# The scores' maximum taken from SBUF, and a pair of PSUM banks held as two tiles

## The chip, the core and the metric

The kernel runs on one core of one Trainium2 chip. The metric is the device time of one execution in microseconds (us); the time of a kernel is the median of its runs. Engine names are those of the profile: PE is the tensor engine's matmul, PEld its weight load, DVE the vector engine, ACT the scalar engine, POOL GpSimd, SP the engine that issues transfers. A PSUM bank holds 512 float32 values in each of 128 partitions, and the kernel uses all eight.

## The reference

Two attentions follow each other per batch and head, then an expert layer follows. All data are float32, with 8 batches, 8 heads, 576 rows, head dimension 64, and 32 packed rows (`p`).

```python
def sm_attn(qq, kk, vv):
    s = scale * np.matmul(qq, kk.transpose(0, 1, 3, 2))
    s = s - np.max(s, axis=-1, keepdims=True)
    a = np.exp(s)
    a = a / (np.sum(a, axis=-1, keepdims=True) + 1e-09)
    return np.matmul(a, vv)
p_packed = sm_attn(p, k, v)
out = sm_attn(q, p_packed, p_packed)
```

The result, as 4608 tokens of 512 values, goes through `h = x @ w_in` (512 by 2048), `g = h * clip(h + 3, 0, 6) / 6` and `g @ w_out` (2048 by 512).

## The kernel before

**The work.** The kernel never forms the attention output. For each batch it makes M, the product of the packed rows and `w_in` (`u_m`), and multiplies it with the second attention's weights (`first_product`, L929) to get h. The gate (`gate_into`, L940 on ACT and L941 on DVE) and the second product with `w_out` (`product`, L969) follow. Float32 operands are parted into a high and a low part in a reduced format (`split`, L946 on ACT and L947 mostly on POOL), and three products of the parts stand for one. From the second chunk of batch 1 on, the second products of most slices go by pairs (`moe_pairs`) with sums of weights that `combine` (L1071 to L1095) makes during batch 1.

**The attention of a batch**, for batches 1 to 7, is a chain of generators. `u_s1` makes the scores of p against k. It has two halves of 288 columns and two parities of heads (`x`), so a half fills a pair of banks, one bank for each parity, with eight products (L350, in `each_head`). For each bank ACT copies the 288 columns to the SBUF tile `e` (L385), and DVE takes their maximum into one column of `mx` (L387). After both halves DVE joins the two maxima and scales them (L391), ACT takes the exponential in place (L398), and DVE makes the reciprocal of the sum (L402, L404). `u_ets` turns e with PE transposes (L440, copies L444), `u_pvs` multiplies with v (L470, L474), `u_ppt` turns the packed rows, and `u_s2` makes the second scores and their softmax (L494 to L524). `u_m` makes a quarter of M in a pair of banks and parts it (`m_hi` L537 on ACT, `m_lo` L539 on DVE).

**The banks.** In the steady stage four banks are accumulators (`ps_o`), two are h (`ps_h`), and two are the attention's pair (`ps_a`). That pair comes from `att_pair`, which in the steady stage gives the two halves of one tile of two banks under one tag with one buffer; before it, `att_pair` gives two separate one-bank tiles of a pool with two buffers. Where the scores' two halves are made at once (batch 1), the second pair is a two-bank tile of `ps_h0` (`ps_w`), the tile that also takes the next first product of `first_moe` (L607). A tile's buffer is handed on when all readers of the tile are done, and the build adds the semaphores.

**The order of the work.** The first stage (batch 0 and batch 1's attention, until the pools change) has its order on all five engines written out in `PLAN`: each token advances one generator by one `yield`. `S` tokens advance `u_s1` of batch 1, which makes both halves at once. The second half's banks come first there. After it, `fill` advances the next batch's attention by `STAGES` beside the expert steps of the present one, and the build's planner orders the instructions on each engine by a model of their times. Only the groups of L350 and L470 have their order on PE fixed, and `behind_gates` keeps what a fill issues behind the product and gate of the step. A quarter of `w_in` is fetched again for each `u_m` from batch 2 on (`w_again`, issued on SP), and a fetch waits until the quarter before has been read.

Of the kernel before, what the change touches and what calls it, by code (L numbers as in the profile page):

```python
# [10 lines left out]
F32 = mybir.dt.float32  # L11
# [5 lines left out]
ALU = mybir.AluOpType  # L17
AX = mybir.AxisListType
# [59 lines left out]
def packed_attention_moe(  # L78
# [17 lines left out]
    nc = tc.nc  # L96
    B, H, S, D = q.shape
    NPK = p.shape[2]
    DM, DF = w_in.shape
    P = 128  # L100
# [10 lines left out]
    scale = 1.0 / float(D) ** 0.5  # L111
# [119 lines left out]
    def att_ps():  # L231
        return spare_ps(0) if steady else ps_a.tile([P, 512], F32, name="ps1", tag="att")

    def att_pair():

        if not steady:
            return [att_ps() for _ in range(2)]
        t = ps_a.tile([P, 2, 512], F32, name="ps2", tag="att")
        return [t[:, x] for x in range(2)]

    state, steady = {}, []

# [93 lines left out]
    def each_head(rows, *rounds):  # L336

        banks = [spare_pair() if i else att_pair() for i in range(len(rounds))]  # L340
        with tc.manual_schedule(engines={mybir.EngineType.PE}), tc.high_priority():
            for pair, cols in reversed(list(zip(banks, rounds))):
                for a in (range(NPAIR - 1, -1, -1) if steady else range(NPAIR)):
                    for x in (1, 0):
                        half = slice(64 * x, 64 * x + 64)
                        c = cols(a, half)
                        n = 1
                        for m in c.shape[1:]:
                            n *= m
                        nc.tensor.matmul(  # L350
                            pair[x][NPK * a:NPK * a + NPK, :n], rows[half, a], c, start=True, stop=True
                        )
        return banks

    def scores(lhs, rhs, *halves):
        def cols(hf):
            hs = slice(hf * HS, (hf + 1) * HS)
            return lambda a, half: rhs[a][half].rearrange("p t i -> p (t i)")[:, hs]

        return [[s[:, :HS] for s in pair] for pair in each_head(lhs, *(cols(hf) for hf in halves))]  # L360

    def both_halves(at_once, lhs, rhs):

        if at_once:
            done = scores(lhs, rhs, 0, 1)
            yield None
            yield from ((hf, done[hf]) for hf in ((0, 1) if steady else (1, 0)))
        else:
            for hf in range(2):
                done = scores(lhs, rhs, hf)  # L370
                yield None
                yield hf, done[0]

    def u_s1(b):
        kt = [state.pop(("k", b, a)) for a in range(NPAIR)]
        pt = state.pop(("p", b))
        e = [ap.tile([P, NST * P], F32, name="e", tag="e", bufs=4) for _ in range(2)]
        mx = [sm.tile([P, 2], F32, name="mx") for _ in range(2)]
        for part in both_halves(b == 1, pt, kt):
            if part is None:  # L380
                yield 1
                continue
            hf, banks = part
            for x, s in enumerate(banks):
                nc.scalar.copy(out=e[x][:, hf * HS:(hf + 1) * HS], in_=s)  # L385
                yield 1
                nc.vector.reduce_max(out=mx[x][:, hf:hf + 1], in_=s, axis=AX.X)  # L387
                yield None if x else 1
        for x in range(2):
            nb = sm.tile([P, 1], F32, name="nb")  # L390
            nc.vector.tensor_scalar(  # L391
                out=nb, in0=mx[x][:, 0:1], scalar1=mx[x][:, 1:2], scalar2=-scale, op0=ALU.max, op1=ALU.mult
            )
            yield 1
            den = sm.tile([P, 1], F32, name="den")
            rinv = sm.tile([P, 1], F32, name="rinv")
            state["e", b, x] = (e[x], rinv)
            nc.scalar.activation(  # L398
                out=e[x][:, :S], in_=e[x][:, :S], func=AF.Exp, bias=nb, scale=scale, accum_out=den
            )  # L400
            yield
            nc.vector.tensor_scalar_add(den, den, 1e-9)  # L402
            yield 1
            nc.vector.reciprocal(rinv, den)  # L404
            yield 1
# [25 lines left out]
    def u_ets(b):  # L431

        e = [state["e", b, x][0] for x in range(2)]
        nc.vector.tensor_copy(out=e[0][:, S:], in_=e[1][:, 4 * P:S])
        yield 1
        et = [ap.tile([P, NST * P], F32, name="et", tag="e", bufs=4) for _ in range(2)]
        pair = att_pair()
        for x in range(2):
            for c in range(4):
                nc.tensor.transpose(  # L440
                    out=pair[x][:, c * P:(c + 1) * P], in_=e[x][:, c * P:(c + 1) * P], identity=ident
                )
            yield 1
            nc.scalar.copy(out=et[x][:, :4 * P], in_=pair[x])  # L444
            yield
        ps = att_ps()
        nc.tensor.transpose(out=ps[:, :P], in_=e[0][:, 4 * P:], identity=ident)
        yield 1
        nc.vector.tensor_copy(out=et[0][:, 4 * P:], in_=ps[:, :P])
        state["et", b] = et  # L450
        yield

    def u_pvs(b):

        rinv = [state.pop(("e", b, x))[1] for x in range(2)]
        et = state.pop(("et", b))
        low = state.pop(("v", b))
        high = [state.pop(("v_high", b, i)) for i in range(2)]
        pair = att_pair()
        rest = et[0][:, 4 * P:]  # L460
        with tc.manual_schedule(engines={mybir.EngineType.PE}), tc.high_priority():
            for c in range(NST):
                for x in range(2):
                    for a in range(NPAIR):
                        cols = slice(NPK * a, NPK * a + NPK)
                        if c < 4:
                            l, r = et[x][:, c * P:(c + 1) * P][:, cols], high[a // 2][:, a % 2, c] if x else low[:, a, c]
                        else:
                            l, r = rest[64 * x:64 * x + REM, cols], low[64 * x:64 * x + REM, a, c]
                        nc.tensor.matmul(pair[x][cols, :D], l, r, start=(c == 0), stop=(c == NST - 1))  # L470
        yield
        pn = state["pn", b] = ap.tile([P, 2, D], F32, name="pn", tag="pn", bufs=1)
        for x in range(2):
            nc.vector.tensor_scalar_mul(pn[:, x], pair[x][:, :D], rinv[x])  # L474
            yield 1
# [103 lines left out]
    def attention(b):  # L579

        yield from coarse(u_s1(b))
        turn("q", b, 0)
        load("q", b, 2)
        yield
        turn("q", b, 1)
        load("q", b, 3)
        yield
        yield
        turn("q", b, 2)
        load_v_high(b, 0)  # L590
        yield
        turn("q", b, 3)
        load_v_high(b, 1)
        yield
        yield from coarse(u_ets(b))
        yield from coarse(u_pvs(b))
        yield
        yield from coarse(u_ppt(b))
# [712 lines left out]
    def next_attention(chains, b):  # L1311


        def once(part):
            part()
            yield

        chains["lp"] = once(lambda: load_p(b))
        chains["tp"] = once(lambda: transpose_p(b))
        for a in range(NPAIR):  # L1320
            for which in "kq":
                chains[f"l{which}{a}"] = once(lambda which=which, a=a: load(which, b, a))
                chains[f"t{which}{a}"] = once(lambda which=which, a=a: turn(which, b, a))
        chains["S"] = u_s1(b)
        chains["lv"] = once(lambda: load_v_low(b))
        for i in range(2):
            chains[f"lw{i}"] = once(lambda i=i: load_v_high(b, i))
        chains["E"] = u_ets(b)
        chains["V"] = u_pvs(b)
        chains["T"] = u_ppt(b)  # L1330
        chains["Z"] = u_s2(b)
        chains["M"] = u_m(b, 0)
# [17 lines left out]
    with tc.manual_schedule(engines=HAND):  # L1350
        for name in PLAN.split():
            if name == "upper":
                upper.close()
                ps_a = upper.enter_context(tc.tile_pool(name="ps_a0", bufs=2, space=bass.MemoryType.PSUM))
# [11 lines left out]
    ps_a = ctx.enter_context(tc.tile_pool(name="ps_a", bufs=1, space=bass.MemoryType.PSUM))  # L1366
# [103 lines left out]
```

## Time and profile before

| what | value |
|---|---|
| time, median of 3 runs | 710.08 us (709.35 to 710.96) |
| the profiled execution's own time | 711.58 us |
| its span, first to last instruction | 709.8 us |
| PE busy | 690.0 us, 97% |
| PEld busy | 593.8 us, 84% |
| DVE busy | 531.0 us, 75% |
| ACT busy | 429.3 us, 60% |
| POOL busy | 354.5 us, 50% |
| chain that ended last, by engine | PE 87%, DVE 6%, DMA 3%, ACT 2% |
| mean granted PE clock | 0.99 |

A row of the timeline has the start in us, the duration in us, engine, line, operation, the tile written and the tiles read, their shapes, and in brackets the engine's idle time before it and what ended it. A row of the waits has the waiting engine, tile and line, what it waited for, the total in us, how often, and the longest. A row on a line's instructions has the shortest, the median and the longest duration in ns and the first and last start. PE's matmuls overlap, so the start of the next tells more than the end of the last.

### The profile page before, as it was taken

Reading aid. Unit: us, or ns where it says so; the run is one execution under the profiler, and the core shown is the slowest. Engines: PE = TensorE matmul, PEld = TensorE weight load, DVE = VectorE, ACT = ScalarE, POOL = GpSimd, SP = SyncE. Lnnn points to the kernel's source line nnn. Section 1 sums busy time; section 2 is a strip of 40 time slices with the busy share of each in tenths; the row PEclk is TensorE's granted clock in tenths of the full one; section 3 lists DMA queues with packets and bytes.
Section 4 is the critical chain, followed back from the end, with each engine's and each line's share of the span. In section 5 each row is a group of like instructions: output and inputs, shape, how many; then the busy total and the mean of one; then the engine's idle time right before and its main releaser. Section 6 shows DMA issues by size and latency. Waiting matters only on the chain.

```text
span 709.8 us, 16077 instructions
## 1 busy us (share of the span) xinstructions
PE 690.0 (97%) x5906; PEld 593.8 (84%) x5906; DVE 531.0 (75%) x1169; ACT 429.3 (60%) x1013; POOL 354.5 (50%) x539
## 2 busy tenths in 40 slices
PE   6699999999998999999999999999999999999997
PEld 5487876888877988899798998889888998889997
DVE  3888788687899769885598867888488867975453
ACT  4798876556556656566466655657366664756453
POOL 1455642555453454475453544556354444547553
PEclk9699999999999999999999999999999999999999
DMA  9969952955328655464454647375543745331030
GB/s 264 341 152 275 215 150 110 266 149 121 109 105 210 165 141 210 116 168 89 118 206 128 160 104 233 120 157 130 127 165 119 166 123 179 119 135 46 31 104 30
DMA packets 199102, 107.48 MB, mean 151 GB/s; under 512 B 173424, under 2 KB 185200, under 8 KB 195440
## 3 DMA queue, kind: packets, MB, share of 16 engines
q1 hardware_dynamic: 198480, 106.26, 53.9%
q8 instruction: 46, 0.75, 0.5%
q14 instruction: 32, 0.26, 0.1%
q10 hardware_dynamic: 544, 0.20, 0.1%
HBM read 89.65 MB, written 16.78 MB: 150 GB/s over the span
## 4 chain that ended last, share of the span: by engine, by line
PE 87%; DVE 6%; DMA 3%; ACT 2%; issue 1%; SPq 0%; POOL 0%; DVEq 0%; ACTq 0%
PE acc L969 47%; PE ps_hh L929 23%; PE ps L350 6%; PE ps_h L607 4%; PE ps L969 2%; PE ps L470 1%; DMA w_again<-w_kept 1%; PE ps L440 1%; DMA room<-in_moe_w_in_dram 1%; DVE wt L1076 1%; PE ps_t L678 1%; DMA k_nat<-in_k_dram 1%; PE ps L273 1%; DVE t L941 1%; PE ps_w L720 1%
## 5 line engine op out<-in xcount | busy, mean ns | idle before, releaser
L929 PE MATMUL ps_hh<-a_hi,m_hi 128*128 128x320 f32 (+1 forms) x448 | 133.8, 299 | 1.7 <-PE acc L969 0.8
L929 PE MATMUL ps_hh<-a_lo,m_hi 128*128 128x320 f32 (+1 forms) x448 | 133.4, 298 | 0.0
L929 PE MATMUL ps_hh<-a_hi,m_lo 128*128 128x320 f32 (+1 forms) x448 | 132.9, 297 | 0.0
L941 DVE SCALAR_TENSOR_TENSOR t<-t,ps_hh 128x320 f32<-128x320 f32 (+1 forms) x148 | 66.1, 446 | 60.3 <-ACT t L940 59.6
L947 POOL TENSOR_TENSOR gf<-tb,gf 128x256 fp32r<-128x256 f32 x76 | 64.3, 847 | 84.3 <-ACT gf L946 48.9
L969 PE MATMUL acc<-wo_hi,g 128*128 128x512 f32 x288 | 103.3, 401 | 0.0
L940 ACT ACTIVATE t<-ps_hh,three 128x320 f32<-128x320 f32 (+1 forms) x148 | 73.8, 500 | 37.3 <-PE ps_hh L929 30.0
L929 PEld LDWEIGHTS ps_hh<-a_hi,m_hi 128*128 128x128 f32 x448 | 84.6, 189 | 8.3 <-issue 3.0
L929 PEld LDWEIGHTS ps_hh<-a_lo,m_hi 128*128 128x128 f32 x448 | 84.7, 189 | 6.6 <-issue 3.5
L929 PEld LDWEIGHTS ps_hh<-a_hi,m_lo 128*128 128x128 f32 x448 | 84.6, 189 | 2.9 <-issue 2.5
L947 POOL TENSOR_TENSOR g<-t,g 128x256 fp32r<-128x256 f32 x72 | 56.3, 783 | 45.4 <-ACT g L946 26.2
L969 PE MATMUL acc<-wt,ga 128*128 128x256 f32 x456 | 74.1, 284 | 0.3 <-ACT ga L946 0.3
L969 PE MATMUL acc<-wo_hi,ge 128*128 128x256 f32 x304 | 71.3, 285 | 0.0
L947 POOL TENSOR_TENSOR ga<-t,ga 128x256 fp32r<-128x256 f32 x76 | 62.4, 821 | 13.9 <-ACT ga L946 12.6
L969 PEld LDWEIGHTS acc<-wt,ga 128*128 128x128 f32 x456 | 63.0, 190 | 2.7 <-ACT ga L946 1.5
L969 PEld LDWEIGHTS acc<-wo_hi,g 128*128 128x128 f32 x288 | 52.8, 188 | 13.9 <-POOL g L947 4.2
L969 PEld LDWEIGHTS acc<-wo_hi,ge 128*128 128x128 f32 x304 | 53.0, 190 | 7.9 <-DVE t L941 2.5
L965 POOL COPY bnd<-t 128x64 f32<-128x64 f32 x76 | 23.0, 302 | 70.8 <-DVE t L941 65.8
L969 PE MATMUL acc<-wo_lo,g 128*128 128x512 f32 x144 | 56.9, 395 | 0.0
L555 DVE STREAM_TRANSPOSE tr<-nat 128x576 f32<-128x576 f32 x56 | 42.3, 763 | 14.3 <-DMA nat<-in_q_dram 10.8
L940 ACT ACTIVATE tb<-ps_hh,three 128x256 f32<-128x256 f32 (+1 forms) x76 | 37.9, 498 | 21.8 <-PE ps_hh L929 19.8
L947 POOL TENSOR_TENSOR edge<-bnd,edge 128x256 fp32r<-128x256 f32 (+1 forms) x50 | 32.7, 659 | 32.5 <-ACT edge L946 32.5
(222 smaller groups left out, 1837.6 us busy)
## 6 DMA issues: line engine op xcount, KB each, us to landing
w_again<-w_kept SPq DMA_DIRECT2D x24, 1024.0 KB, 4.9
wt<-t_kept SPq DMA_DIRECT2D x24, 768.0 KB, 5.6
out_dram<-osb SPq DMA_DIRECT2D x33, 256.0 KB, 2.4
nat<-in_k_dram SPq DMA_DIRECT2D x112, 72.0 KB, 3.0
nat<-in_q_dram SPq DMA_DIRECT2D x112, 72.0 KB, 2.7
raw_in<-in_moe_w_in_dram SPq DMA_DIRECT2D x10, 512.0 KB, 5.7
raw_out<-in_moe_w_out_dram SPq DMA_DIRECT2D x10, 512.0 KB, 4.9
w_kept<-w_in_sb SPq DMA_DIRECT2D x4, 1024.0 KB, 9.2
```

Of the source, the lines that this page charges most:

```text
L273: nc.tensor.matmul(banks[x][NPK * a:NPK * a + NPK, :n * P], state["pp"][half, NPAIR * x + a], cols[half, :, a], start=True, stop=True,)
L350: nc.tensor.matmul(pair[x][NPK * a:NPK * a + NPK, :n], rows[half, a], c, start=True, stop=True)
L440: nc.tensor.transpose(out=pair[x][:, c * P:(c + 1) * P], in_=e[x][:, c * P:(c + 1) * P], identity=ident)
L470: nc.tensor.matmul(pair[x][cols, :D], l, r, start=(c == 0), stop=(c == NST - 1))
L555: nc.vector.transpose(out=t, in_=state.pop(("nat", which, b, a)))
L607: nc.tensor.matmul(h[:, hf, :HS], mm[:, g, fs], aa[:, hf * HS:(hf + 1) * HS], start=(g == 0 and i == 0), stop=(g == NG - 1 and i == 2),)
L929: state["first"] = nc.tensor.matmul(h[:, :n], mm[:, g, fs], aa[:, t0:t0 + n], start=(g == 0 and i == 0), stop=(g == NG - 1 and i == 2),)
L940: state["relu"] = nc.scalar.activation(out=t[:, :n], in_=h, func=AF.Relu, bias=three)
L941: state["gate"] = nc.vector.scalar_tensor_tensor(out=t[:, :n], in0=t[:, :n], scalar=6.0, in1=h, op0=ALU.min, op1=ALU.mult)
L947: engine.tensor_sub(out=lo, in0=x, in1=hi.bitcast(F32))
L965: nc.gpsimd.tensor_copy(out=bnd[:, f, side * REM:side * REM + REM], in_=t[:, boff:boff + REM])
L969: nc.tensor.matmul(out, lhs[x], rhs[y], start=first and i == 0, stop=last and i == 2, skip_group_check=True)
```

## The change

Three things change.

- `att_pair` gives, in the steady stage, two tiles of one bank with a tag of their own each (`att0`, `att1`), instead of the two halves of one tile of two banks. Users of the pair are `each_head` (scores and M), `u_ets`, `u_pvs` and, in the last batch, `edge_step`.
- `u_s1` no longer reads the banks with DVE. The copies to `e` stay. Once the second half of a parity is copied, one maximum over all 576 columns is taken from `e`. The number of `yield`s is the same, so a token of `PLAN` that took a maximum of the first copied half now issues nothing.
- The scaling of the maximum reads one column and multiplies by a constant.

```diff
         if not steady:
             return [att_ps() for _ in range(2)]
-        t = ps_a.tile([P, 2, 512], F32, name="ps2", tag="att")
-        return [t[:, x] for x in range(2)]
+        return [ps_a.tile([P, 512], F32, name="ps2", tag=f"att{x}") for x in range(2)]
...
         mx = [sm.tile([P, 2], F32, name="mx") for _ in range(2)]
+        copied = 0
         for part in both_halves(b == 1, pt, kt):
             if part is None:
                 yield 1
                 continue
             hf, banks = part
+            copied += 1
             for x, s in enumerate(banks):
                 nc.scalar.copy(out=e[x][:, hf * HS:(hf + 1) * HS], in_=s)
                 yield 1
-                nc.vector.reduce_max(out=mx[x][:, hf:hf + 1], in_=s, axis=AX.X)
+                if copied == 2:
+                    nc.vector.reduce_max(out=mx[x][:, 0:1], in_=e[x][:, :S], axis=AX.X)
                 yield None if x else 1
         for x in range(2):
             nb = sm.tile([P, 1], F32, name="nb")
-            nc.vector.tensor_scalar(
-                out=nb, in0=mx[x][:, 0:1], scalar1=mx[x][:, 1:2], scalar2=-scale, op0=ALU.max, op1=ALU.mult
-            )
+            nc.vector.tensor_scalar(out=nb, in0=mx[x][:, 0:1], scalar1=-scale, scalar2=None, op0=ALU.mult)
```

## The prediction

> **What bounds the kernel now.** I read the page's busy shares first, then the waits of TensorE (PE), then windows of 18 us over the whole span, then the timeline around the score maxima, and last the instructions of line 387 and those that read its tile.
>
> ```profile
> PE 690.0 (97%) x5906; PEld 593.8 (84%) x5906; DVE 531.0 (75%) x1169; ACT 429.3 (60%) x1013; POOL 354.5 (50%) x539
> ```
> ```profile
> PE ps_t L678 <- DMA k_nat<-in_k_dram: 5.1, 1, 5.1
> ...
> PE ps L350 <- DMA w_again<-w_kept: 1.1, 1, 1.1
> ...
> PE ps_hh L929 <- PE acc L969: 0.8, 1, 0.8
> PE ps_h L607 <- DVE mx L387: 0.7, 1, 0.7
> PE ps_hh L929 <- DVE t L941: 0.6, 1, 0.6
> ```
> The columns of a wait are total us, times, longest. PE is idle for 709.8 - 690.0 = 19.8 us in all, much of it before the first data land (the 5.1 us row). Only one of its waits names the line that the change touches: 0.7 us behind the maximum, L387. The windows say where the rest can lie:
>
> ```profile
> 216.00:234.00 18.00, 16.00 (x144) 13.78 (x143) 15.32 (x38) 11.87 (x31) 8.49 (x13) 1.00 0.93 226
> 234.00:252.00 18.00, 18.00 (x144) 16.59 (x143) 12.23 (x33) 10.74 (x29) 7.91 (x12) 1.00 0.61 153
> ...
> 522.00:540.00 18.00, 18.00 (x159) 17.03 (x158) 17.70 (x36) 11.14 (x30) 10.24 (x13) 1.00 0.54 203
> ...
> 666.00:684.00 18.00, 18.00 (x126) 16.77 (x125) 9.53 (x22) 8.50 (x23) 8.33 (x14) 1.00 0.18 61
> ```
> After the stretch come busy us of PE, its weight loads, DVE, ACT and POOL, then granted clock, share and rate of DMA. In all 25 windows from 234 to 684 us PE is at 18.00 (the first, one from between and the last are shown); even where DVE is at 17.70, PE does not wait. There a faster maximum has nothing to give. The gain must come out of the first 234 us or not at all.
>
> **The change part by part.** First, the chain that the maxima make today. In the first stage, whose order on all engines is written out in PLAN, the scores of batch 1 lie in four banks, two of them in the two-bank tile ps_w that first_moe's next product needs:
>
> ```profile
> 56.51 0.40 ACT L385 COPY e<-ps_w 128x288 f32<-128x288 f32 x1 [0.34 <-PE ps_w L350]
> 57.43 0.40 ACT L385 COPY e<-ps_w 128x288 f32<-128x288 f32 x1 [0.52 <-DVE mx L387]
> 57.73 0.41 ACT L385 COPY e<-ps 128x288 f32<-128x288 f32 x1
> ```
> ```profile
> 56.94 0.46 DVE L387 TENSOR_REDUCE mx<-ps_w 128x1 f32<-128x288 f32 x1 [0.39 <-ACT e L385]
> 57.86 0.46 DVE L387 TENSOR_REDUCE mx<-ps_w 128x1 f32<-128x288 f32 x1 [0.47 <-ACT e L385]
> ```
> ```profile
> 57.38 0.40 PE L969 MATMUL acc<-wo_hi,gl 128*128 128x512 f32 x1
> 58.47 0.37 PE L607 MATMUL ps_h<-a_hi,m_hi 128*128 128x288 f32 x1 [0.68 <-DVE mx L387]
> ```
> Copy, maximum, copy, maximum run one after the other, and the next product waits for the last: 0.68 us. The second copy reads the other bank, and still starts 0.03 us after the first maximum ends (56.94 + 0.46 = 57.40). The Trainium skill, "PSUM — Partial Sum Buffer", Terms, says that two engines may not be on one bank at once, reads against reads included. By that only the pair on one bank has to be kept apart; the trace shows the pair across banks kept apart too, so the order here comes from sharing a tile.
>
> With no maximum on the banks, the second copy follows the first. Two copies need 2 x 0.40 us from 56.51, so the banks are free by 57.31 at the latest. PE ends its earlier work at 57.38 + 0.40 = 57.78, which is later, so the whole wait goes: 0.68 us. What is late next? PLAN's other two maxima, now over 576 elements, come later on DVE in their old places:
>
> ```profile
> 62.93 0.42 DVE L387 TENSOR_REDUCE mx<-ps 128x1 f32<-128x288 f32 x1
> 63.27 0.84 DVE L1270 TENSOR_TENSOR gl<-t,gh 128x512 fp32r<-128x512 f32 x1
> ```
> ```profile
> 64.93 0.39 PE L969 MATMUL acc<-wo_hi,gl 128*128 128x512 f32 x1
> ```
> The price of the long maximum is not in the trace under that shape. Its two nearest rows read 576 elements, one from PSUM into one column, one from SBUF into 18:
>
> ```profile
> L387 DVE TENSOR_REDUCE mx<-ps x26: 411/446/459, 62.9 to 574.9; 128x1 f32<-128x288 f32 x26
> ...
> L502 DVE TENSOR_REDUCE mx<-z x14: 709/738/746, 98.1 to 609.3; 128x18 f32<-128x576 f32 x14
> ...
> L745 DVE TENSOR_REDUCE mx<-ps_w x2: 756/756/756, 12.5 to 13.6; 128x1 f32<-128x576 f32 x2
> ```
> I take 738 ns, from the row that also reads SBUF; the ends are 709 and 756. The Trainium skill, "VectorE: DVE Perf Modes", "The TRN2 errata", gives 120 cycles plus the length from PSUM and 58 plus the length from SBUF, at 0.96 GHz; an estimate from that page is 425 ns for the short maximum (the trace has 446) and 660 ns for the long one. By the page a batch would save 4 x 425 - 2 x 660 = 380 ns on DVE; no row here shows a one-column maximum from SBUF.
>
> So each long maximum takes 738 - 446 = 0.29 us more at its place. The product of low parts at 63.27 moves 0.29 us back, and forward by what ACT and DVE gained earlier: the second copy starts at 56.91 at the latest instead of 57.43, so 0.52 us. It still ends by 63.27 + 0.84 + 0.29 - 0.52 = 63.88, and PE, 0.68 us early, wants it at 64.93 - 0.68 = 64.25. That holds with 0.37 us to spare. A load could still eat the gain later in the stage:
>
> ```profile
> 89.32 0.67 ACT L193 ACTIVATE raw_in<-raw_in 128x512 f32<-128x512 f32 x1 [1.06 <-DMA raw_in<-in_moe_w_in_dram]
> ```
> ```profile
> 92.38 1.30 POOL L203 TENSOR_TENSOR w_in_sb<-w_in_sb,raw_in 128x512 int32<-128x512 int32 x1 [0.42 <-DVE w_in_sb L199]
> ```
> ```profile
> 94.47 1.09 PE L273 MATMUL ps<-w_in_sb,pp 64*32 64x512 f32 x16
> ```
> If the weights do not land earlier, POOL still ends at 93.68 and PE would ask at 94.47 - 0.68 = 93.79. It is close, 0.11 us, and holds. I take 0.68 us for the first stage, with 0 and 0.68 as its ends.
>
> Second, the steady stage, where a planner in the build orders everything but a few PE groups. Batch 4's scores:
>
> ```profile
> 312.64 0.40 ACT L385 COPY e<-ps 128x288 f32<-128x288 f32 x1
> ...
> 314.83 0.40 ACT L385 COPY e<-ps 128x288 f32<-128x288 f32 x1
> ```
> ```profile
> 314.35 0.44 DVE L387 TENSOR_REDUCE mx<-ps 128x1 f32<-128x288 f32 x1
> 315.26 0.46 DVE L387 TENSOR_REDUCE mx<-ps 128x1 f32<-128x288 f32 x1 [0.46 <-ACT e L385]
> ```
> ```profile
> 317.82 0.72 PE L350 MATMUL ps<-tr,p_tr 64*32 64x288 f32 x16
> ```
> The first maximum queues behind DVE's gates, the second copy behind it, and the second half of the scores (317.82) behind both. Afterwards the banks are free at about 312.64 + 2 x 0.40 = 313.44 instead of 315.72, some 2.3 us sooner, and the planner may put the second half that much earlier. PE has other products meanwhile and never waits here, so for five of the six steady batches this is worth nothing; the cover is the queue of expert products, and the windows at 18.00 show that it suffices.
>
> The new wait in the steady stage is that of a long maximum for the copy of its second half. On DVE's queue the gates (L941) stand behind it, and behind those the casts and PE's second products. Today's maxima wait for a copy too, so it is a longer one of the same kind: +0.29 us each at the second half, -0.45 us each at the first.
>
> For batch 2, prepared while PE does have waits, there may be something:
>
> ```profile
> 194.62 0.38 PE L929 MATMUL ps_hh<-a_hi,m_hi 128*128 128x256 f32 x1 [0.64 <-DVE t L941]
> ...
> 216.72 0.39 PE L929 MATMUL ps_hh<-a_hi,m_hi 128*128 128x256 f32 x1 [0.30 <-DVE tb L941]
> 218.15 0.38 PE L969 MATMUL acc<-wo_hi,gf 128*128 128x256 f32 x1 [0.22 <-POOL gf L947]
> 218.87 0.74 PE L969 MATMUL acc<-wt,ga 128*128 128x256 f32 x4 [0.33 <-ACT ga L946]
> 220.87 1.09 PE L350 MATMUL ps<-w_again,pps 64*32 64x512 f32 x16 [1.14 <-DMA w_again<-w_kept]
> ```
> The 0.64 us wait is for DVE, which is the crowded engine there. A batch's maxima cost 4 x 446 = 1.78 us today and 2 x 738 = 1.48 us after: 0.30 us less work ahead of that gate. I take these 0.30 us off the 0.64; the ends are 0 (the slack is used up by a transfer on the way) and 0.64.
>
> Third, the split of the pair into two one-bank tiles, apart from the scores. The new quarter of M is parted by ACT and DVE in turn, and the shared tile makes them alternate:
>
> ```profile
> ACT m_hi L537 <- DVE m_lo L539: 5.8, 14, 1.1
> ```
> These 5.8 us lie on ACT, which is 60% busy, and the transfer that PE awaits at 220.87 does not hang on them alone. I take 0, with the four waits at 194 to 221 us as the bound (0.64 + 0.30 + 0.22 + 0.33 + 1.14 = 2.63 us). The scaling of the maximum (L391) only loses an operand and the transposes of u_ets no longer await each other's copy; PE is covered there: 0.
>
> Sum: 0.68 + 0.30 = 0.98 us. The profiled execution took 711.58 us, 709.80 of it span; it would take 710.6. The median of the three runs is 1.50 us lower, 710.08, and what I forecast for it is 710.08 - 0.98 = 709.1. What a measurement here can tell from no change is about 0.2%, 1.42 us, so this counts as the same.
>
> **The rivals.** *The handover to batch 2 is freed.* If the earlier banks let the planner ask for w_again sooner and clear DVE, all of the 2.63 us go besides the 0.68: 710.08 - 3.31 = 706.8. For it: those waits are the only ones left, and two of them are for engines that the change relieves. Against: 1.14 us of them is a transfer whose start hangs on SP's queue, which no maximum touches. Chance 0.27.
>
> *Long maxima hold up the gates.* A long maximum can't start before the second half's copy, and DVE stands still behind it. If the planner puts it directly ahead of a gate, that gate is 2 x 0.29 = 0.58 us late in each of six steady batches, and PE loses 3.5 us, less the 0.68: 710.08 + 2.8 = 712.9. It decides where PE's queue of products covers less than 0.58 us. For it: at 194.62 the cover was already below zero, and DVE stands at 17.70 of 18 us in one window. Against: after 234 us no gate was ever late for PE. A new order by the planner that is simply worse costs about the same. Chance 0.21.
>
> *The first stage's gain is lost to the loads* (0.11 us of room above), and the DVE work hides: 710.1. Chance 0.10. It also covers that the copies stay chained for another reason and the change does not do what it says.
>
> **How the numbers follow.** My forecast has the remaining 0.42, from 0.3 to 1.7 us gained. About 0.07 of it lies beyond 1.42 us, so faster is 0.27 + 0.07 = 0.34; the same is 0.35 + 0.10 = 0.45; slower is 0.21. The range leaves out half of the slower case and a little below the freed handover: 706.5 to 711.6. The forecast's own is 708.4 to 709.8.
>
> **What would show it.** Right: L387 14 times near 0.74 us, no wait of PE L607 behind mx, two copies of L385 within 0.5 us of each other, a smaller wait near 194 us, PE still at 18.00 after 234. Wrong: new waits of PE for L941 or for POOL and ACT parts after 234 us, a longer wait for w_again, or a wait for w_in_sb near 94 us that takes the 0.68 us back.

## The result and the profile after

The changed kernel takes 720.77 us, the median of six runs (718.25 to 723.45). The kernel before takes 710.52 us beside it (709.21 to 713.07). The ratio is 1.0134, with a 95% interval of 1.0113 to 1.0155: slower by 1.3%, about 9.5 us by the ratio (the medians are 10.3 us apart), where 709.1 us had been forecast, and far above the range's 711.6. The profiled execution took 720.54 us, 718.8 of it span, against 711.58 and 709.8 before, so the two traces hold about 9 us of difference.

The page of the kernel after, its busy shares:

```profile
PE 697.9 (97%) x5906; PEld 596.2 (83%) x5906; DVE 526.1 (73%) x1155; ACT 425.6 (59%) x1013; POOL 360.2 (50%) x539
```

PE runs the same 5906 instructions and is *busy* 7.9 us longer (697.9 against 690.0). Its idle time grew by only 1.1 us (718.8 - 697.9 = 20.9, against 19.8). So most of the loss is not in waits: the same products take PE longer. Some 1.7 us of it is a stretch at half clock, told of at the end; the rest is not. DVE has 14 instructions and 4.9 us less, and it helped nothing.

The waits of PE after (total, times, longest):

```profile
PE ps_t L678 <- DMA k_nat<-in_k_dram: 5.2, 1, 5.2
...
PE ps L349 <- DMA w_again<-w_kept: 2.0, 1, 2.0
...
PE ps_hh L929 <- DVE tb L941: 0.9, 1, 0.9
PE acc L969 <- ACT osb_j L1181: 0.8, 2, 0.4
...
PE ps_hh L929 <- DVE t L941: 0.6, 1, 0.6
```

The 0.7 us of L607 behind the maximum is gone, as forecast. The waits for w_again (1.1 before) and for tb (0.3) have grown, and osb_j is new.

The windows of the kernel after, the same four as before (columns as in the prediction):

```profile
216.00:234.00 18.00, 15.17 (x123) 13.61 (x131) 14.70 (x32) 9.74 (x25) 8.14 (x12) 0.91 0.90 222
234.00:252.00 18.00, 18.00 (x165) 16.23 (x166) 11.88 (x33) 11.31 (x30) 7.47 (x11) 1.00 0.52 139
...
522.00:540.00 18.00, 17.62 (x144) 16.05 (x143) 14.24 (x29) 10.91 (x30) 9.92 (x13) 1.00 0.42 162
666.00:684.00 18.00, 18.00 (x113) 16.27 (x113) 8.54 (x22) 7.25 (x20) 8.56 (x16) 1.00 0.08 30
```

The first has lost 0.83 us of PE and shows a granted clock of 0.91. In most of the others PE is still at 18.00, yet time is being lost there. That shows when the start of one and the same first product is compared in the two traces:

| start before, us | 119.9 | 169.6 | 209.4 | 230.5 | 270.0 | 361 | 436.6 | 528 | 603 | end |
|---|---|---|---|---|---|---|---|---|---|---|
| after minus before, us | -1.58 | -0.66 | -0.51 | +1.83 | +4.84 | +4.40 | +7.0 | +6.64 | +9.64 | +8.95 |

Of the lead at 119.9 us, 1.15 us stood already at the first scores of batch 1 (they start at 54.54 us after and 55.69 before), where the change has had no part yet. From there to the end 8.95 + 1.58 = 10.5 us are lost, in steps around each batch's attention, most of them where PE reads 18.00.

What PE does in such a step can be read from the timeline. A group of eight products of M (two instructions for each, so x16), in the kernel before and then in the same quarter of batch 3 in the kernel after:

```profile
270.42 1.09 PE L350 MATMUL ps<-w_again,pps 64*32 64x512 f32 x16
271.44 0.41 PE L929 MATMUL ps_hh<-a_hi,m_lo 128*128 128x320 f32 x1
271.69 0.31 PE L929 MATMUL ps_hh<-a_hi,m_hi 128*128 128x320 f32 x1
271.83 0.31 PE L929 MATMUL ps_hh<-a_lo,m_hi 128*128 128x320 f32 x1
```
```profile
270.32 1.04 PE L349 MATMUL ps<-w_again,pps 64*32 64x512 f32 x2
271.29 0.39 PE L969 MATMUL acc<-wo_hi,gf 128*128 128x256 f32 x1
271.52 0.52 PE L969 MATMUL acc<-wt,gf 128*128 128x256 f32 x3
271.96 1.08 PE L349 MATMUL ps<-w_again,pps 64*32 64x512 f32 x14
272.98 0.38 PE L969 MATMUL acc<-wo_hi,ge 128*128 128x256 f32 x1
```

Read the starts. Before, eight products keep PE from 270.42 to 271.44: 1.02 us. After, one product alone keeps it from 270.32 to 271.29, 0.97 us, and the other seven from 271.96 to 272.98, again 1.02 us. Each product uses a 64 by 32 part of the array, and eight run beside each other. One alone costs about what eight do, and a full-array product behind it does not run beside it. All of it is booked as busy. The Trainium skill, "TensorEngine Tiling (Array Packing)", Key Properties, says that tiles of one mode run in parallel and that a change of the tiling mode drains the array; the trace fits both, with 1.02 us for the eight beside 0.97 us for the one, and the full-array product starting only after that.

Why did the group break? All eight write the pair's two banks in turn. With one tile, the first product waits for the same event as the last, the release of the whole tile, so nothing was gained by issuing it alone. With two tiles the first product needs one bank only, and the second needs the other, which is released at another time. The planner may issue the first as soon as its own bank is free and put expert products behind it. This is read from the code; the experiments below test it. The order of PE shows the breaks: M of batches 2 to 7 came in 24 separate pieces and now comes in 27, the products with v of batches 1 to 7 in 7 and now 14. (Pieces are counted so in all that follows, those of the scores for batches 1 to 7.) A group with v in the kernel after, with an expert product between its first and its other chunks:

```profile
161.13 0.32 PE L470 MATMUL ps<-v_nat,et 128*32 128x64 f32 x8
161.38 0.42 PE L929 MATMUL ps_hh<-a_hi,m_hi 128*128 128x320 f32 x1
161.73 0.32 PE L470 MATMUL ps<-v_high,et 128*32 128x64 f32 x8
161.87 0.29 PE L470 MATMUL ps<-v_nat,et 128*32 128x64 f32 x8
```

Inside the group the next chunk follows 0.14 us later (161.73 to 161.87); the lone first chunk keeps PE for 0.25 us, and the product behind it for 0.35 us. In the rows of before at 271.69 and later such a product keeps PE for 0.14 us. That is about 0.3 us lost on a broken group with v. Three heads of M and seven more pieces of v come to 3 x 0.97 + 7 x 0.3 = 5.0 us; with the 1.7 us at half clock this is 6.7 of the 7.9 us by which PE is busy longer.

### The profile page after: what moved, and what is told of

It reads as the page before. It is cut to its first block, busy times and chain, and to the rows that moved or that the text cites. A ratio compares the mean times of both kernels' runs of the same rounds, so it can differ in the third digit from the quotient of the medians.

```text
span 718.8 us, 16062 instructions
## 1 busy us (share of the span) xinstructions
PE 697.9 (97%) x5906; PEld 596.2 (83%) x5906; DVE 526.1 (73%) x1155; ACT 425.6 (59%) x1013; POOL 360.2 (50%) x539
## 4 chain that ended last, share of the span: by engine, by line
PE 84%; DMA 6%; DVE 5%; ACT 3%; POOL 1%; issue 1%; SPq 0%; ACTq 0%; POOLq 0%
PE acc L969 46%; PE ps_hh L929 24%; PE ps L349 6%; PE ps_h L607 3%; DMA raw_in<-in_moe_w_in_dram 2%; PE ps L969 2%; DMA raw_out<-in_moe_w_out_dram 1%; PE ps L470 1%; DMA w_again<-w_kept 1%; PE ps L440 1%; PE ps L272 1%; DMA room<-in_moe_w_in_dram 1%; DMA p_nat<-in_p_dram 1%; DVE t L941 0%; DVE z L494 0%
## 5 line engine op out<-in xcount | busy, mean ns | idle before, releaser
L947 POOL TENSOR_TENSOR ga<-t,ga 128x256 fp32r<-128x256 f32 x76 | 64.5, 848 | 17.9 <-ACT ga L946 15.0
```

What stands on the lines that cost most here:

```text
L947: engine.tensor_sub(out=lo, in0=x, in1=hi.bitcast(F32))
```

## The experiments

The theory: the split of the pair breaks PE's groups, and lone heads of groups cost PE time while it counts as busy. The rivals: the long maxima hold up DVE's gates; PE's idle time at 216 to 221 us brings the half clock seen there; the first stage or a planner's worse order makes it. All ratios are to the kernel before on the same chip, whose medians in the three batches of runs were 711.63, 712.69 and 712.16 us; a per cent is 7.1 us.

**The maximum alone.** The changed kernel with the shared tile put back.

```diff
-        return [ps_a.tile([P, 512], F32, name="ps2", tag=f"att{x}") for x in range(2)]
+        t = ps_a.tile([P, 2, 512], F32, name="ps2", tag="att")
+        return [t[:, x] for x in range(2)]
```

> The maximum from SBUF alone, the pair of banks still one tile of two banks. Theory A (one-bank tiles let the first product of a PE group go ahead of the rest, and a lone product costs PE nearly as much as the group): no group of M is broken, so about the kernel before, 709 to 711 us, with the first stage 0.7 us earlier. Rival B (the longer maxima change the order on DVE and ACT, so that PE waits for gates and for w_again): most of the 10 us is still there, 717 to 721 us.

Measured: 713.04 us, ratio 1.0023 (1.0008 to 1.0039). M comes in 24 pieces, v in 9. That lies between the two expectations: the maximum from SBUF loses 0.2%; it isn't a gain, and it isn't the 1.3%.

**The split alone.** The kernel before with two one-bank tiles.

```diff
-        t = ps_a.tile([P, 2, 512], F32, name="ps2", tag="att")
-        return [t[:, x] for x in range(2)]
+        return [ps_a.tile([P, 512], F32, name="ps2", tag=f"att{x}") for x in range(2)]
```

> The two one-bank tiles alone, the maxima still taken on the banks. Theory A: three M products and about six groups of packed values go ahead of their groups, 3 x 0.97 + 6 x 0.3 = 4.7 us and what follows from it, 715 to 720 us. Rival B: as before, 709 to 711 us.

Measured: 727.84 us, ratio 1.0217 (1.0186 to 1.0248). The split alone loses more than the whole change, and more than the 715 to 720 us expected: M in 27 pieces, v in 13, and here v's heads cost waits as well. The waits of PE in this kernel, and its timeline:

```profile
PE ps L469 <- DMA v_high<-in_v_dram: 3.1, 6, 1.5
PE ps L349 <- DMA w_again<-w_kept: 2.2, 1, 2.2
```
```profile
504.81 0.32 PE L469 MATMUL ps<-v_nat,et 128*32 128x64 f32 x8
...
505.22 0.23 PE L469 MATMUL ps<-v_high,et 128*32 128x64 f32 x2
506.96 0.25 PE L469 MATMUL ps<-v_high,et 128*32 128x64 f32 x2 [1.51 <-DMA v_high<-in_v_dram]
```

A head of v (which reads v_nat, there already) goes ahead; the products in fixed order behind it then hold PE for 1.51 us until the last of v_high has landed.

**The groups made whole again, the change kept.** Only the order within the groups is turned, so that the first product is one that needs what is ready last: the other parity first in the products with v, and in the three quarters of M that were broken.

```diff
-    def each_head(rows, *rounds):
+    def each_head(rows, *rounds, order=(1, 0)):
...
-                    for x in (1, 0):
+                    for x in order:
...
-                for x in range(2):
+                for x in (1, 0):
...
-        rounds = each_head(pps[b % 2], *(cols(n) for n in ns))
+        rounds = each_head(pps[b % 2], *(cols(n) for n in ns), order=(0, 1) if b in (3, 5, 7) and ns == (NCH - 2,) else (1, 0))
```

> The changed kernel with the order of the two parities turned round in the product with v and in the first M product of batches 3, 5 and 7, so that each group's first product is the one whose bank comes free last; the built order then has those groups whole. Theory A: the 4.7 us of the broken groups come back, 714 to 716.5 us; what is left is the longer wait for w_again and the half clock behind it. Rival B: nothing changes, 719 to 722 us.

Measured: 715.85 us, ratio 1.0068 (1.0046 to 1.009). M is back at 24 pieces and v at 8, and half of the loss is gone: 0.66%, 4.7 us, a difference of two ratios that are each known to 0.2%. In its profile PE is busy 692.3 us, 5.6 us less than in the kernel after, of which the half clock is 1.7. The same products, with the same sizes and the same tiles, in another order. The quarter of batch 3 in this kernel, whole again:

```profile
271.07 1.09 PE L349 MATMUL ps<-w_again,pps 64*32 64x512 f32 x16
272.09 0.41 PE L929 MATMUL ps_hh<-a_hi,m_hi 128*128 128x320 f32 x1
```

**The dose: more groups broken.** The changed kernel with the other parity first in all scores and all of M, which leaves more of their first products free to go alone, and with the turned order of the products with v.

```diff
-                    for x in (1, 0):
+                    for x in (0, 1):
...
-                for x in range(2):
+                for x in (1, 0):
```

> The changed kernel with the parities turned round in all groups: six more M groups, six first scores and six second scores are broken, two groups of v fewer. Theory A, with 0.97 us for a lone M product and about 0.6 us for a lone score product: 6 x 0.97 + 12 x 0.6 = 13 us more than the changed kernel, 730 to 736 us. Rival B: 719 to 723 us.

Measured: 735.26 us, ratio 1.0339 (1.0314 to 1.0363), so 2.05% or 14.6 us more than the change. M comes in 33 pieces (6 more), each of the two scores in 19 (12 more, with 13 and 13 before). A head of M and a head of the scores in this kernel:

```profile
267.76 0.67 PE L349 MATMUL ps<-tr,pps 64*32 64x288 f32 x2
268.36 0.39 PE L969 MATMUL acc<-wo_hi,ge 128*128 128x256 f32 x1
268.58 0.28 PE L969 MATMUL acc<-wt,ga 128*128 128x256 f32 x1
268.79 0.71 PE L349 MATMUL ps<-tr,pps 64*32 64x288 f32 x14
...
272.35 1.04 PE L349 MATMUL ps<-w_again,pps 64*32 64x512 f32 x2
273.32 0.39 PE L969 MATMUL acc<-wo_hi,gf 128*128 128x256 f32 x1
```

A head of the scores keeps PE for 0.60 us (267.76 to 268.36), one of M for 0.97 us (272.35 to 273.32). The sum is 12 x 0.60 + 6 x 0.97 = 13.0 us; a seventh head of M, in batch 1 at 125.11 us, stands outside the count of pieces and makes it 14.0 us. Measured were 14.6 us, although v comes in 12 pieces instead of 14. PE is busy 712.1 us in this profile, 14.2 us more than in the kernel after, and its trace has no half clock after the first 40 us. The price of a head, and that PE pays it in full, is shown by this dose.

**The two orders one by one.** First the v groups alone, then M alone, in the changed kernel.

```diff
-                for x in range(2):
+                for x in (1, 0):
```

> The changed kernel with the parities turned round in the product with v alone: six groups of v whole again, the three M groups still broken. If a lone group head costs what the trace shows between starts (0.25 us and some 0.1 us at the next two products), 6 x 0.3 = 2 us come back: 718 to 719.5 us. If only M counts, 720 to 721 us.

Measured: 717.97 us, ratio 1.009 (1.0064 to 1.0115), 0.44% or 3.1 us less than the change, just clear of the noise of the two ratios. v comes in 8 pieces, M still in 27. The half clock, below, does not occur in this profile.

```diff
-        rounds = each_head(pps[b % 2], *(cols(n) for n in ns))
+        rounds = each_head(pps[b % 2], *(cols(n) for n in ns), order=(0, 1) if b in (3, 5, 7) and ns == (NCH - 2,) else (1, 0))
```

(with the parameter `order` of the third experiment)

> The changed kernel with the parities turned round in the first M product of batches 3, 5 and 7 alone: M whole, the groups of v still broken. With 0.97 us for a lone M product, 3 us come back: 717 to 718.5 us. If only the groups of v count, 720 to 721 us.

Measured: 719.4 us, ratio 1.0104 (1.0075 to 1.0133), 0.30% or 2.1 us less than the change, above the 717 to 718.5 us expected; 3 heads x 0.97 us = 2.9 us is the price by the rows. The interval of this ratio overlaps that of the change, so the part of M alone isn't clear of noise here; its price rests on the rows and the dose. M comes in 24 pieces, v in 14. The two together (0.74%) agree with the 0.66% of both at once, within the intervals.

**The control.** The kernel before, with its shared tile, and all the turned orders of the third experiment, of which this is the line for v:

```diff
-                for x in range(2):
+                for x in (1, 0):
```

> A control: the kernel before with the same turned parities as in e3_whole_groups (product with v, first M product of batches 3, 5 and 7). With the shared tile all groups are whole in either order, so if the turning helps only by keeping groups whole, there is no difference from the kernel before (within 0.2%). If the order by itself were worth the 0.66% between the changed kernel and e3, this would be 4 to 5 us faster.

Measured: 711.49 against 712.16 us, ratio 0.9997 (0.9981 to 1.0013). The order by itself is worth nothing; it counts only where the banks are separate tiles.

**The turned orders with the split alone.** The kernel before with one-bank tiles and the same orders.

```diff
-        t = ps_a.tile([P, 2, 512], F32, name="ps2", tag="att")
-        return [t[:, x] for x in range(2)]
+        return [ps_a.tile([P, 512], F32, name="ps2", tag=f"att{x}") for x in range(2)]
...
-                for x in range(2):
+                for x in (1, 0):
```

> The two one-bank tiles alone, maxima on the banks, with the turned parities: M is whole, ten groups of v instead of thirteen. Theory A: of the 2.2% of the split alone, the 1.0% of three M heads, broken groups of v and the waits for v_high inside them come back; 716 to 721 us. If the loss of the split alone is something else, 726 to 729 us.

Measured: 722.38 us, ratio 1.0144 (1.0121 to 1.0168): 0.7% less than the split alone, and above the 716 to 721 us that were expected. M is at 24 pieces, v at 10. What PE still waits for in this kernel:

```profile
PE ps_hh L928 <- DVE tb L940: 2.2, 4, 0.9
...
PE ps L349 <- DMA w_again<-w_kept: 1.8, 1, 1.8
PE ps L469 <- DMA v_high<-in_v_dram: 1.8, 4, 0.9
```

So unbroken groups are not the whole of what the shared tile gives. With the split and the maxima on the banks PE begins v before v_high has landed; neither the kernel before nor the kernel after has such a wait, so it comes with this order of the work and not with the split as such.

**The maximum for batch 1 alone, and for the others alone.** Both with the shared tile; the count `copied` and the scaling of one column go with the batches that have the new maximum.

```diff
-                nc.vector.reduce_max(out=mx[x][:, hf:hf + 1], in_=s, axis=AX.X)
+                if b == 1:
+                    if copied == 2:
+                        nc.vector.reduce_max(out=mx[x][:, 0:1], in_=e[x][:, :S], axis=AX.X)
+                else:
+                    nc.vector.reduce_max(out=mx[x][:, hf:hf + 1], in_=s, axis=AX.X)
```

> The kernel before with the maximum from SBUF in batch 1 alone, where the order is written out; the tile of two banks stays. If the 0.68 us of the prediction stays won, 0.7 us below before, 710.9 beside 711.6. If the loads of the first stage take it back (a raw_in lands at 89.2 us whatever PE does), no difference.

Measured: 711.92 against 712.69 us, ratio 1.0 (0.9983 to 1.0017). The medians are 0.77 us apart, but the interval is 1.2 us wide to either side and holds no change as well as the 0.68 us, so these times decide nothing. The trace of the maximum alone, in the next section, shows where the gain goes.

The other one has `b > 1` in the condition's place:

```diff
-                if b == 1:
+                if b > 1:
```

> The kernel before with the maximum from SBUF in batches 2 to 7 alone; the tile of two banks stays. If the small loss of the maximum alone (0.2%) comes from the planner's order in the steady stage (two groups of v broken, gates later at 216 us), it is here too, 712.5 to 714 us. If it comes from the first stage, 711 to 712 us.

Measured: 713.53 us, ratio 1.0023 (1.0005 to 1.004). So the steady batches by themselves show the 0.23% of the maximum alone. What part of it is the work and what part the clock stays open: by their mean granted clocks and spans these runs spend 17.2 us at half clock on average, an estimate, and the runs of the kernel before beside them 14.5 us. That difference could be worth as much as 1.3 us, or 0.2%, if PE were the limit all that time.

**Is the maximum's 0.23% two broken v groups?** The maximum alone (shared tile), with the order of the products with v turned.

```diff
-                for x in range(2):
+                for x in (1, 0):
```

> The maximum from SBUF alone on the shared tile, with the parities turned in the product with v, so that one of its two extra heads is gone. Theory A: 0.3 us better than the maximum alone, ratio 1.001 to 1.002 to the kernel before; a version that beats the kernel before would be below 0.998, which I do not expect.

Measured: 713.64 us, ratio 1.0021 (1.0007 to 1.0034), with v in 8 pieces instead of 9. The loss of 0.2% stays. The 0.3 us of one head is 0.04% and too small to be told here; by the same price two heads are 0.6 us, 0.08%, so they are not the most of it. No version that was run beats the kernel before.

## Why the prediction was wrong

**The step that failed** is "Third, the split of the pair into two one-bank tiles", which was taken at 0, with "PE is covered there: 0" for the scaling and the transposes; the products with v have no term at all. It looked at what the split *frees* and bounded the gain by PE's waits. That a freer product may be issued earlier, alone, and that this costs, was in none of its terms. The rivals had only a sentence on "a new order by the planner that is simply worse", put at 712.9 us, with no place and no price of its own. The runs put in its place: +2.2% for the split without the rest, +1.3% with it, and 0.66% (4.7 us) given back when only the order within the groups is turned.

**"There a faster maximum has nothing to give"** (after 234 us, PE at 18.00) was right as to gains, and misled as to losses. A full window bounds what removing a wait can bring. It says nothing on how dense the work in it is: 10.5 us were lost between 120 us and the end, most of it under 18.00.

**The first stage, 0.68 us.** The wait of 0.68 us went, and for the reason given. ACT and PE in the kernel after:

```profile
55.36 0.70 ACT L386 COPY e<-ps_w 128x288 f32<-128x288 f32 x2 [0.38 <-PE ps_w L349]
```
```profile
56.23 0.39 PE L969 MATMUL acc<-wo_hi,gl 128*128 128x512 f32 x1
56.47 0.29 PE L607 MATMUL ps_h<-a_hi,m_hi 128*128 128x288 f32 x1
```

The two copies run back to back (x2 within 0.70 us), and L607 follows its predecessor with no wait. It starts 0.24 us after it, where the kernel before has 1.09 us between the two, so 0.85 us are won here: the prediction counted from the end of the product before (57.78), and here the next one starts 0.15 us ahead of that end (56.23 + 0.39 = 56.62). Then the third rival took most of it back, by another way than the one named. The load (`raw_in`, L193) is awaited until 89.32 us before and 88.64 after. In the kernel after PE's lead over the kernel before grows from 1.15 to 2.07 us at the scores and is 1.41 us at 97 us. In the run with the maximum alone it grows from 1.69 to 2.61 us, the load lands where it did before, and the lead behind it is 0.85 us. ACT, DVE and PE of that run:

```profile
89.20 0.65 ACT L193 ACTIVATE raw_in<-raw_in 128x512 f32<-128x512 f32 x1 [3.45 <-DMA raw_in<-in_moe_w_in_dram]
```
```profile
89.88 0.43 DVE L199 TENSOR_SCALAR w_in_sb<-raw_in 128x512 int32<-128x512 int32 x1 [2.50 <-ACT raw_in L193]
90.22 0.28 DVE L483 COPY pps<-ps 128x128 f32<-128x128 f32 x1
```
```profile
90.56 0.72 PE L350 MATMUL ps_w<-tr,pps 64*32 64x288 f32 x16 [1.30 <-DVE pps L483]
```

ACT waits 3.45 us for the load (1.06 before); DVE's shift waits for ACT; the copy of the packed rows stands behind it on DVE's queue; and PE's second scores wait 1.30 us for that copy. The prediction had "0.11 us of room", reckoned along POOL and the product at 94.47. It did not look at who stands behind L199 on DVE, which comes earlier.

**"0.30 for batch 2"** was wrong, and the handover to batch 2 got worse. PE in the kernel after:

```profile
194.08 0.39 PE L929 MATMUL ps_hh<-a_hi,m_hi 128*128 128x256 f32 x1 [0.64 <-DVE t L941]
...
216.80 0.39 PE L929 MATMUL ps_hh<-a_hi,m_hi 128*128 128x256 f32 x1 [0.89 <-DVE tb L941]
217.02 0.28 PE L929 MATMUL ps_hh<-a_lo,m_hi 128*128 128x256 f32 x1
217.14 0.27 PE L929 MATMUL ps_hh<-a_hi,m_lo 128*128 128x256 f32 x1
...
220.53 1.31 PE L349 MATMUL ps<-w_again,pps 64*32 64x512 f32 x16 [2.03 <-DMA w_again<-w_kept]
```

The 0.64 us at 194 us stayed as it was; the 0.30 and 1.14 us became 0.89 and 2.03 us. With the maximum alone the wait for `t` at that place is gone (0.2 us for POOL is left), as the term would have it, but a new one of 0.52 us for ACT's output copy (`osb`, near 180 us) stands before it.

**The long maximum** was sized right. Its tile in the kernel after (shortest, median and longest ns):

```profile
L389 DVE TENSOR_REDUCE mx<-e x14: 704/734/753, 61.2 to 581.3; 128x1 f32<-128x576 f32 x14
```

734 ns against the 738 taken. The rival that long maxima hold up the gates had the right sign; its mechanism is shown in part only. The three kernels with the steady maximum from SBUF on the shared tile all wait near 216 to 220 us for the gate `tb`, 0.76 to 0.78 us where the kernel before waits 0.30, and near 180 us for `osb`, 0.52 to 1.65 us where it doesn't wait; other waits shrink, and what that comes to is not told apart here. The maximum from SBUF shows 0.23%, and the change in its whole-group form another 0.45% (1.0068 against 1.0023). In that form there are waits of PE for tb (1.6 us in three) and for ge (0.6 us), which fit gates that come late. Which of them the new order makes, and which the maxima, stays open.

**What the parts come to**, in per cent of the time: 0.23 the maximum, 0.66 broken groups, 0.45 the split with whole groups. They sum to the 1.34 because each is a difference between two runs of a chain; they are not separate causes, and each is known to 0.2 or 0.3. The 0.66 is shown, by the turned orders, the control and the dose; what makes the 0.23 and the 0.45 is not. Without the maximum the split with whole groups costs 1.44, not 0.45, so the two parts of the change act on each other through the planner's order.

## What to carry to other kernels

A tile that spans two PSUM banks was also a fence here: it made a group of small-array products wait for one event and so go in one piece. Before freeing such a tile, count the groups in the built order of PE, before and after, and price a lone head from a row (the start of the next instruction, not the duration). Where PE is at 100% busy, ask not only what could wait less but what could come to run less densely.

## What was not expected of the hardware

**A lone small-array product costs PE what a full group does:** 0.97 us against 1.02 us for seven or eight products with 512 columns, 0.60 against 0.64 us for seven with 288 (from 268.79 to the next start at 269.43).

**Half clock after short idle times.** Every profile has a stretch at half clock near the start (13.65 us from 24.38 us before, 17.07 us from 19.89 us after); this is about later ones. In the 216 to 234 us window after, the granted clock is 0.91; in the trace it is 0.5 for 3.41 us from 221.27 us. (18 - 3.41 / 2) / 18 = 0.91. PE in the kernel after, inside that stretch:

```profile
223.22 0.41 PE L929 MATMUL ps_hh<-a_hi,m_hi 128*128 128x256 f32 x1
223.43 0.41 PE L929 MATMUL ps_hh<-a_lo,m_hi 128*128 128x256 f32 x1
```

These products start 0.21 us apart; at full clock those at 217.02 and 217.14 us start 0.12 us apart. So about 1.7 us are lost. The half clock is not what makes the change slow: of its six runs two have a mean granted clock of 0.990 and 0.993, no lower than that of the kernel before in its profile (0.990), and they take 718.25 and 719.56 us, still 7.7 and 9.0 us above its median; the four at 0.986 and 0.987 take 720.54 to 723.45 us. The profiles of the split alone (at 221.38 and 508.1 us), of M alone made whole (221.03) and of the split with whole groups (222.37) show it too; the kernel before and the other experiments don't. PE's idle times just before were 0.89 and 2.03 us after, 0.88 and 1.22 us where M alone was whole, and a single 1.51 us in the second case of the split alone; with v alone whole 0.86 and 1.53 us brought no drop, nor did 0.90 and 1.18 us with all groups whole. No single idle time separates them, and what sets it off stays open. The Trainium skill, "TensorE: Matmul & The Clock Gate", Part 1, gives a free-running window of 3413 ns and half clock after an idle one; the length agrees with 3.41 us. Its rule of thumb, in "HAM oscillation — how this bites in real kernels", warns of idle gaps over some 3.4 us; here the drop came where the longest gap was 1.2 to 2.2 us, and the measurement decides.
